# Batches 0 to 2 in 1 KB packets with TensorE transposes, a fixed order of loads, casting weight loads and a later FFN, in an attention and FFN kernel

## The chip, the cores and the metric

The kernel runs on one core of one Trainium2 chip. The metric is device time in microseconds (us) of one execution; lower is better.

Engine names in the profile: PE is TensorE's matmuls, PEld its weight loads, DVE is VectorE, ACT is ScalarE, POOL is GpSimd, SP is SyncE, which here only issues DMAs. "L293" is line 293 of that run's kernel, so line numbers differ from kernel to kernel.

## The reference

Block-causal attention for 8 batches of 8 heads, 576 tokens and 64 channels, then a gated FFN over all 4,608 tokens.

```python
scores = (q @ k.transpose(0, 1, 3, 2)) / sqrt(64)        # q, k, v: (8, 8, 576, 64) float32
scores = where(block_i >= block_j, scores, -1e9)         # blocks of 64 tokens
attn = softmax(scores);  x = (attn @ v).transpose(0, 2, 1, 3).reshape(4608, 512)
out = (maximum(x @ w_gate, 0) * (x @ w_val)) @ w_out     # 512 -> 1536 -> 512
```

## The kernel before

All matmuls are in bf16. The work of attention is cut in 32 *pairs* (two heads of a batch; pair r is head pair r % 4 of batch r // 4). The FFN is a generator of 1,296 matmuls of 512 columns, 144 for each batch and 144 for the collected 64-token tails, and `ffn(n)` sends the next n of them between the pieces of attention. Only TensorE's program order is written by hand; the order on the other engines is made by the scheduler of the language, which ranks the instructions when the program is built.

Batch 0 is loaded as float32 on the SP queue and cast by VectorE; batches 1 to 7 come through casting DMAs from GpSimd's queue and DMA transposes. In both, a packet is one token of one head, 256 B in HBM. Weights are loaded as float32 and cast by whichever engine the scheduler picks.

```python
def load_batch(b):                       # batches 1 to 7
    m, tl = new_bf()                     # bufs=1
    for t, src in enumerate((q, k, v)):
        for c in range(NCH):
            ...
            nc.gpsimd.dma_start(dst, src[b, :, 128*c : 128*c+n, :].rearrange("h p d -> p h d"))
        if t < 2:
            nc.sync.dma_start_transpose((qTm, kTm)[t][b % 2]..., m[t]...)
            ...
def to_xT_dma(r):                        # result of a pair, transposed for the FFN
    nc.sync.dma_start_transpose(xT_of(b)[:, hp, :]..., xnat[:, 0:4, :]...)
...
m0, t0 = load_first_batch()
for i in range(4): load_w_in(i)          # float32 on SP, then nc.any.tensor_copy
...                                      # pairs 0 to 3, with TensorE transposes
load_batch(1)
for i in range(3): load_w_out(i)
ffn(64)
for r in range(4, 4 * B):
    a = [2, 2, 2, 4] if b == 1 else [8, 4, 8, 16]
    scores_1(r); ffn(a[0])
    if r > 4: head_av(r-1, 0); ffn(a[1]); head_av(r-1, 1); to_xT_dma(r-1)
    else: ffn(a[1])
    if hp == 0 and b + 1 < B: load_batch(b + 1)
    ffn(a[2]); scores_2(r); ffn(a[3])
```

The softmax here doesn't subtract the row's maximum and nothing guards it: scores larger than these inputs give would overflow.

Of the kernel before, what the change touches and what calls it, by code (L numbers as in the profile page):

```python
# [10 lines left out]
FP = mybir.dt.float32  # L11
BF = mybir.dt.bfloat16
# [5 lines left out]
def kernel(  # L18
# [10 lines left out]
    nc = tc.nc  # L29

    B, H, S, D = q.shape
# [12 lines left out]
    sb = ctx.enter_context(tc.tile_pool(name="sb", bufs=1))  # L44
# [10 lines left out]
    ident = consts.tile([128, 128], BF)  # L55
# [13 lines left out]
    for i in range(2):  # L69
# [4 lines left out]
        nc.gpsimd.memset(v_bf[i][:, 0:4, :, 64:65], 1.0)  # L74
        nc.gpsimd.memset(v_bf[i][0:64, 4, :, 64:65], 1.0)


    def new_bf():
        m = [sb.tile([128, 4, 512], BF, name=n, bufs=1) for n in ("q_bf", "k_bf")]
        t = [sb.tile([64, 512], BF, name=n, bufs=1) for n in ("q_bt", "k_bt")]  # L80
        return m, t

    def load_first_batch():
        m, tl = new_bf()
        for hp in range(4):
            st = sb.tile([128, 3, 5, 128], FP, name="stage", bufs=4)
            hs = slice(128 * hp, 128 * hp + 128)
            for t, src in enumerate((q, k, v)):
                for hh in range(2):
                    nc.sync.dma_start(  # L90
                        st[:, t, 0:4, 64 * hh : 64 * hh + 64],
                        src[0, 2 * hp + hh, 0:512, :].rearrange(
                            "(c p) d -> p c d", p=128
                        ),
                    )
                nc.sync.dma_start(
                    st[0:64, t, 4, :].rearrange("p (h d) -> p h d", h=2),
                    src[0, 2 * hp : 2 * hp + 2, 512:576, :].rearrange("h p d -> p h d"),
                )
                if t < 2:  # L100
                    nc.vector.tensor_copy(m[t][:, :, hs], st[:, t, 0:4, :])
                    nc.vector.tensor_copy(tl[t][:, hs], st[0:64, t, 4, :])
                else:
                    h2 = slice(2 * hp, 2 * hp + 2)
                    sv = st[:, t, :, :].rearrange("p c (h d) -> p c h d", h=2)
                    nc.vector.tensor_copy(v_bf[0][:, 0:4, h2, 0:64], sv[:, 0:4])
                    nc.vector.tensor_copy(v_bf[0][0:64, 4, h2, 0:64], sv[0:64, 4])
        return m, tl

    def load_batch(b):  # L110
        m, tl = new_bf()
# [16 lines left out]
                )  # L128
                nc.sync.dma_start_transpose((qTt, kTt)[t][b % 2][:, 0:4, :], tl[t])  # L129

    def load_w_in(i):
        for dst, src in ((wg, moe_w_gate), (wv, moe_w_val)):
            st = sb.tile([128, 4, 384], FP, name="stage", bufs=4)
            nc.sync.dma_start(
                st,
                src[:, 384 * i : 384 * (i + 1)].rearrange("(c p) f -> p c f", p=128),
            )
            nc.any.tensor_copy(dst[i], st)

    def load_w_out(i):  # L140
        st = sb.tile([128, 4, 512], FP, name="stage", bufs=4)
        nc.sync.dma_start(
            st,
            moe_w_out[512 * i : 512 * (i + 1), :].rearrange("(c p) f -> p c f", p=128),
        )
        nc.any.tensor_copy(wo[i], st)


    def pe_transposes(hp, m, tl):
        hs = slice(128 * hp, 128 * hp + 128)  # L150
        for t in range(2):
            tp = psum_ffn.tile([128, 1024], BF, name="ffnp")
            for c in range(4):
                nc.tensor.transpose(
                    tp[:, 128 * c : 128 * c + 128], m[t][:, c, hs], ident
                )
            nc.tensor.transpose(tp[:, 512:576], tl[t][:, hs], ident[:64, :64])
            nc.vector.tensor_copy(
                (qTm, kTm)[t][0][:, :, hp, :],
                tp[:, 0:512].rearrange("p (c n) -> p c n", c=4),  # L160
            )
            nc.vector.tensor_copy((qTt, kTt)[t][0][:, hp, :], tp[:, 512:576])

    def scores(b, hp, pieces):
        sc = psum_sc.tile([128, 2, 512], FP, name="sc")
        for pos, c, main in pieces:
            for hh in range(2):
                ps = slice(64 * hh, 64 * hh + 64)
                n = 512 - 128 * c if main else 64
                o = sc[:, hh, pos : pos + n]  # L170
                if main:
                    o = o.rearrange("p (c n) -> p c n", n=128)
                nc.tensor.matmul(  # L173
                    o,
                    kTm[b % 2][ps, c, hp, :]
                    if c < 4
                    else kTt[b % 2][ps, hp : hp + 2, :].rearrange("p h n -> p (h n)"),
                    qTm[b % 2][ps, c:4, hp, :] if main else qTt[b % 2][ps, hp, :],
                    start=True,
                    stop=True,  # L180
                )
        return sc
# [12 lines left out]
    def scores_2(r):  # L195
        b, hp = divmod(r, 4)
        at = attnT[r % 2]
        sc = scores(b, hp, [(0, 2, True)] + [(256 + 64 * c, c, False) for c in range(4)])
        nc.scalar.activation(at[:, :, 1024:1536], sc, AF.Exp, scale=scale)  # L199
        nc.vector.memset(at[64:128, :, 1024:1088], 0.0)  # L200
        sc = scores(b, hp, [(0, 4, False)])
        nc.scalar.activation(
            at[0:64, :, 1536:1600], sc[0:64, :, 0:64], AF.Exp, scale=scale
        )
# [4 lines left out]
    def head_av(r, hh):  # L209
        b, hp = divmod(r, 4)  # L210
        h = 2 * hp + hh
        at = attnT[r % 2]
        vb = v_bf[b % 2]
        if hh == 0:
            xnats[r] = sb.tile([128, NCH, 128], BF, name="xnat", bufs=3)
        xnat = xnats[r]
        av = psum_av.tile([128, NCH, 65], FP, name="av")
        for p in range(NCH):
            for c in range(p + 1):
                col = BASE[c] + 128 * (p - c) if p < 4 else TAIL + 64 * c  # L220
                nc.tensor.matmul(  # L221
                    av[:, p, :],
                    at[:, hh, col : col + 128],
                    vb[:, c, h, :],
                    start=(p == 0),
                    stop=(c == p),
                    skip_group_check=True,
                )
        recip = sb.tile([128, NCH], FP, name="recip", bufs=4)
        nc.vector.reciprocal(recip, av[:, :, 64])  # L230
        nc.vector.tensor_tensor(  # L231
            out=xnat[:, :, 64 * hh : 64 * hh + 64],
            in0=av[:, :, 0:64],
            in1=recip.to_broadcast([128, NCH, 64]),
            op=AX.mult,
        )
# [16 lines left out]
    def to_xT_dma(r):  # L253
        b, hp = divmod(r, 4)
        xnat = xnats[r]
        nc.sync.dma_start_transpose(
            xT_of(b)[:, hp, :].rearrange("p (c n) -> p c n", c=4),
            xnat[:, 0:4, :].rearrange("p c n -> p (c n)"),
        )
        nc.sync.dma_start_transpose(xTt[:, hp, b : b + 1, :], xnat[0:64, 4, :])  # L260
# [60 lines left out]
    def ffn(n):  # L321
        for _ in range(n):
            if next(gen, 0) == 0:
                return


    m0, t0 = load_first_batch()
    for i in range(4):
        load_w_in(i)

    with tc.manual_schedule(engines={mybir.EngineType.PE}):
        pe_transposes(0, m0, t0)
        for r in range(4):
            scores_1(r)
            if r < 3:
                pe_transposes(r + 1, m0, t0)
            if r > 0:
                head_av(r - 1, 0)
                head_av(r - 1, 1)
            scores_2(r)  # L340
            if r > 0:
                to_xT_pe(r - 1)
        head_av(3, 0)
        head_av(3, 1)
        to_xT_pe(3)
        load_batch(1)
        for i in range(3):
            load_w_out(i)
        ffn(64)
        for r in range(4, 4 * B):  # L350
            b, hp = divmod(r, 4)
            a = [2, 2, 2, 4] if b == 1 else [8, 4, 8, 16]
            scores_1(r)
            ffn(a[0])
            if r > 4:
                head_av(r - 1, 0)
                ffn(a[1])
                head_av(r - 1, 1)
                to_xT_dma(r - 1)
            else:  # L360
                ffn(a[1])
            if hp == 0 and b + 1 < B:
                load_batch(b + 1)
            ffn(a[2])
            scores_2(r)
            ffn(a[3])
        head_av(4 * B - 1, 0)
        ffn(4)
        head_av(4 * B - 1, 1)
        to_xT_dma(4 * B - 1)  # L370
        ffn(10**6)
# [30 lines left out]
```

## Time and profile before

Three runs took 443.13 to 447.69 us, median 444.28; the profiled execution spans 445.2 us.

The page of the kernel before: TensorE's busy time, its busy tenths in 40 slices of 11.1 us, the granted clock in tenths, the busy share of the DMA engines in tenths, and the two data queues (packets, MB, share of 16 engines).

```profile
PE 374.7 (84%) x2844; PEld 180.5 (41%) x2892; DVE 174.8 (39%) x459; ACT 169.6 (38%) x243; POOL 90.8 (20%) x117
...
PE   1467957866199979997999699989999999999995
...
PEclk9999998799599999999999879999999999999999
DMA  9989999999990599059905990492013002002004
...
q0 software_dynamic: 98448, 12.39, 50.0%
q1 hardware_dynamic: 76528, 34.82, 36.2%
```

TensorE is mostly at 9 tenths from slice 11 on (counted from 0), with dips, and mostly below it before. The DMA engines are nearly full for the first 130 us; over the span q0, which casts 256 B to 128 B in each packet, takes half of their time for a quarter of the bytes written (12.39 of 47.66 MB; the page counts a casting packet by its size after the cast). The waits view of the same kernel (who waited for whom: us in total, times, longest):

```profile
PE ffnp L271 <- DMA xT<-xnat: 25.0, 5, 14.2
...
PE sc L173 <- DMA kTm_89<-k_bf: 5.1, 1, 5.1
```

and two lines of its timeline of TensorE (start, us, instruction; in brackets the idle time before it and what ended it):

```profile
106.29 0.81 PE L271 MATMUL ffnp<-xT,wg_75 128*128 128x512 bf16 x3
121.29 0.59 PE L271 MATMUL ffnp<-xT,wg_75 128*128 128x512 bf16 x1 [14.18 <-DMA xT<-xnat]
```

The FFN of batch 1 stood 14.18 us before its fourth matmul, for a transposed result (xT) that came by DMA. Four more such waits came later, of 2.46, 2.58, 3.81 and 1.96 us. The trace's clock records show half rate from 110.3 us, during the long wait, for 13.7 us, and again from 164.9, 209.3 and 253.7 us, at the first three of the later ones, for 3.4, 3.4 and 6.8 us; at the last the record stayed full.

One caution about the clock row: it shows 9 in the first slices because the trace has no clock record before 48.9 us. The matmuls suggest half rate there: four FFN matmuls took 1.75 us at 47.41 us and 1.03 us from 49.00 on.

To follow the time I read the start of the first score matmul of some pairs from the timelines:

| start, us | before |
|---|---|
| pair 0 | 11.97 |
| pair 3 | 35.94 |
| first FFN matmul | 46.13 |
| pair 4 (batch 1) | 66.31 |
| pair 8 (batch 2), 104 FFN matmuls sent | 92.72 |
| pair 12 (batch 3), 248 FFN matmuls sent | 150.71 |
| end | 445.2 |

### The profile page before, as it was taken

To read this page: it belongs to the slowest core of one execution; us is meant where nothing else is said; L and a number is where in the kernel's file an instruction comes from. 1 tells how busy PE (TensorE), PEld (TensorE's weight loads), DVE (VectorE), ACT (ScalarE), POOL (GpSimd) and SP (SyncE) were. 2 spreads that over 40 slices of the span, in tenths; PEclk is the share of its full clock that TensorE was granted. 3 is DMA by queue.
4 is the path that set the end of the run, shared out by engine and by line. 5 is a ranking of instruction groups with operands and counts; after the bars stand their busy time and mean duration, and the time that the engine had idled before them with its cause. 6 is when DMAs were issued, how large, how long until landed. Compare 5 with 4: busy or idle time off the path is not lost.

```text
span 445.2 us, 7281 instructions
## 1 busy us (share of the span) xinstructions
PE 374.7 (84%) x2844; PEld 180.5 (41%) x2892; DVE 174.8 (39%) x459; ACT 169.6 (38%) x243; POOL 90.8 (20%) x117
## 2 busy tenths in 40 slices
PE   1467957866199979997999699989999999999995
PEld 0245423332044434443444244434444444444442
DVE  2565522531044424442444134424444453433331
ACT  1427415732045334533453245425534550330320
POOL 5034333154600181027102610030000000000000
PEclk9999998799599999999999879999999999999999
DMA  9989999999990599059905990492013002002004
GB/s 137 176 253 238 263 155 303 169 132 132 185 95 15 96 179 127 15 113 167 124 13 115 154 134 15 74 157 65 15 38 92 19 16 84 26 0 94 1 0 94
DMA packets 175010, 47.66 MB, mean 107 GB/s; under 512 B 164737, under 2 KB 168833, under 8 KB 174977
## 3 DMA queue, kind: packets, MB, share of 16 engines
q0 software_dynamic: 98448, 12.39, 50.0%
q1 hardware_dynamic: 76528, 34.82, 36.2%
q8 instruction: 22, 0.36, 0.3%
q14 instruction: 12, 0.09, 0.1%
HBM read 37.75 MB, written 9.44 MB: 106 GB/s over the span
## 4 chain that ended last, share of the span: by engine, by line
PE 62%; DMA 20%; issue 5%; SPq 4%; ACT 3%; DVE 3%; POOL 1%; DVEq 0%; ACTq 0%
PE ffnp L283 19%; PE ffnp L271 17%; PE ffnp L299 15%; DMA xT<-xnat 9%; PE av L221 6%; PE sc L173 5%; DMA k_bf<-in_k_dram 5%; DMA stage<-in_moe_w_out_dram 2%; SPq L125 2%; DMA stage<-in_q_dram 2%; DMA xTt<-xnat 2%; DVE xnat L231 1%; SPq L129 1%; SPq L90 1%; ACT gate_sb L280 1%
## 5 line engine op out<-in xcount | busy, mean ns | idle before, releaser
L280 ACT ACTIVATE gate_sb<-ffnp 128x512 bf16<-128x512 f32 x108 | 64.4, 596 | 153.2 <-PE ffnp L271 153.1
L293 DVE TENSOR_TENSOR hT<-gate_sb,ffnp 128x512 bf16<-128x512 bf16 x108 | 74.3, 688 | 84.5 <-PE ffnp L283 79.6
L299 PEld LDWEIGHTS <-hT 128*128 128x128 bf16 x432 | 39.6, 98 | 45.6 <-issue 2.5
L120 POOL DMA_DIRECT2D q_bf<-in_q_dram x28 | 24.5, 892 | 150.9 <-DMA qTm_86<-q_bf 77.1
L271 PE MATMUL ffnp<-xT,wg_75 128*128 128x512 bf16 x89 | 26.1, 405 | 25.8 <-DMA xT<-xnat 25.0
L309 DVE COPY ob<-ffnp 128x512 f32<-128x512 f32 x36 | 24.9, 692 | 38.1 <-PE ffnp L299 24.6
L221 PEld LDWEIGHTS <-attnT_94 128*128 128x128 bf16 x480 | 21.5, 108 | 42.8 <-issue 28.9
L299 PE MATMUL ffnp<-wo_85,hT 128*128 128x512 bf16 x142 | 36.8, 380 | 0.2
L299 PE MATMUL ffnp<-wo_84,hT 128*128 128x512 bf16 x137 | 35.5, 380 | 0.6
L299 PE MATMUL ffnp<-wo_83,hT 128*128 128x512 bf16 x137 | 35.6, 379 | 0.1
L231 DVE TENSOR_TENSOR xnat<-av,recip 128x320 bf16<-128x320 f32 x64 | 31.5, 491 | 4.4 <-DMA xTt<-xnat 2.3
L199 ACT ACTIVATE attnT_94<-sc 128x1024 bf16<-128x1024 f32 x16 | 16.3, 1021 | 36.8 <-PE sc L173 36.8
L283 PE MATMUL ffnp<-xT,wv_79 128*128 128x512 bf16 x96 | 28.7, 428 | 0.0
L188 ACT ACTIVATE attnT_94<-sc 128x1024 bf16<-128x1024 f32 x16 | 16.4, 1023 | 32.2 <-PE sc L173 32.2
L230 DVE RECIPROCAL recip<-av 128x5 f32<-128x5 f32 x64 | 12.3, 193 | 36.9 <-PE av L221 35.9
L120 POOL DMA_DIRECT2D k_bf<-in_k_dram x28 | 24.8, 900 | 8.4 <-DMA kTm_89<-k_bf 4.9
L221 PEld LDWEIGHTS <-attnT_95 128*128 128x128 bf16 x480 | 18.8, 102 | 17.9 <-DVE xnat L231 14.2
L271 PE MATMUL ffnp<-xT,wg_77 128*128 128x512 bf16 x89 | 25.1, 390 | 0.4
L283 PE MATMUL ffnp<-xT,wv_82 128*128 128x512 bf16 x93 | 25.3, 389 | 0.1
L283 PE MATMUL ffnp<-xT,wv_81 128*128 128x512 bf16 x96 | 25.1, 383 | 0.0
L271 PE MATMUL ffnp<-xT,wg_78 128*128 128x512 bf16 x90 | 24.6, 391 | 0.3
L271 PE MATMUL ffnp<-xT,wg_76 128*128 128x512 bf16 x90 | 24.4, 380 | 0.3
(103 smaller groups left out, 423.4 us busy)
## 6 DMA issues: line engine op xcount, KB each, us to landing
out_dram<-ob SPq DMA_DIRECT2D x32, 256.0 KB, 5.7
q_bf<-in_q_dram POOLq DMA_DIRECT2D x28, 128.0 KB, 6.8
k_bf<-in_k_dram POOLq DMA_DIRECT2D x28, 128.0 KB, 9.2
stage<-in_moe_w_gate_dram SPq DMA_DIRECT2D x4, 768.0 KB, 7.7
stage<-in_moe_w_val_dram SPq DMA_DIRECT2D x4, 768.0 KB, 8.5
stage<-in_moe_w_out_dram SPq DMA_DIRECT2D x3, 1024.0 KB, 10.9
v_bf_97<-in_v_dram POOLq DMA_DIRECT2D x16, 128.0 KB, 7.5
v_bf_96<-in_v_dram POOLq DMA_DIRECT2D x12, 128.0 KB, 11.6
```

What stands on the lines that cost most here:

```text
L120: nc.gpsimd.dma_start(dst, src[b, :, 128 * c : 128 * c + n, :].rearrange("h p d -> p h d"),)
L173: nc.tensor.matmul(o, kTm[b % 2][ps, c, hp, :] if c < 4 else kTt[b % 2][ps, hp : hp + 2, :].rearrange("p h n -> p (h n)"), qTm[b % 2][ps, ...
L188: nc.scalar.activation(at[:, :, 0:512], sc, AF.Exp, scale=scale)
L199: nc.scalar.activation(at[:, :, 1024:1536], sc, AF.Exp, scale=scale)
L221: nc.tensor.matmul(av[:, p, :], at[:, hh, col : col + 128], vb[:, c, h, :], start=(p == 0), stop=(c == p), skip_group_check=True,)
L231: nc.vector.tensor_tensor(out=xnat[:, :, 64 * hh : 64 * hh + 64], in0=av[:, :, 0:64], in1=recip.to_broadcast([128, NCH, 64]), op=AX.mult,)
L271: nc.tensor.matmul(gate, wg[i][:, c, fo : fo + 128], x[:, c, :], start=(c == 0), stop=(c == 3),)
L280: nc.scalar.activation(gate_sb, gate, AF.Relu)
L283: nc.tensor.matmul(val, wv[i][:, c, fo : fo + 128], x[:, c, :], start=(c == 0), stop=(c == 3),)
L293: nc.vector.tensor_tensor(out=h, in0=gate_sb, in1=val, op=AX.mult)
L299: nc.tensor.matmul(op, hT[f][:, 128 * s : 128 * (s + 1)], wo[f // 4][:, f % 4, :], start=(f == 0), stop=(f == 11),)
L309: nc.vector.tensor_copy(ob, op)
```

## The change

The intent: feed TensorE earlier and without gaps. Batches 0 to 2 are staged as float32, q and k with four tokens (1 KB) in a packet, and transposed by TensorE; the casts of staged batches are on VectorE. Loads wait for one another in a fixed order: batch 0, input weights, batch 1, output weights, batch 2; a load that waits for an earlier one is called *gated* below. Weights are cast by the DMA itself. The results of pairs 4 to 7 are transposed by TensorE too, instead of by DMA. The FFN runs 20 of its matmuls later (a pair of the steady part sends 36).

```diff
+    def after(ins, other):               # a wait on another engine's or DMA's completion
+        if other is not None: tc.add_manual_dep(ins.ins, other.ins.name, SYNC)
+        return ins
-        m = [sb.tile([128, 4, 512], BF, name=n, bufs=1) for n in ("q_bf", "k_bf")]
+        m = [sb.tile([128, 4, 512], BF, name=n, bufs=2) for n in ("q_bf", "k_bf")]
-    def load_first_batch(): ...          # 256 B packets, batch 0 only
+    def early_load(b, per, gate=None):   # batches 0 to 2
+        ...
+        for h0 in range(0, 8, per):
+            for t, src in enumerate((q, k)):
+                st = new_stage(256 * per)
+                i = nc.sync.dma_start(st.rearrange("p (h n) -> p h n", h=per),
+                    src[b, h0:h1, 0:512, :].rearrange("h (p j) d -> p h (j d)", j=4))
+                after(i, gate)
+            ...
+            for t in range(2):
+                nc.vector.tensor_copy(m[t][...], sts[t]...)       # the cast
+            ... v in 256 B packets, one DMA a head, after(i, gate), cast -> mark
+    def load_w_in(i, gate=None):
-            nc.sync.dma_start(st, ...); nc.any.tensor_copy(dst[i], st)
+            ins = nc.gpsimd.dma_start(dst[i], ...); after(ins, gate)
     ...  load_w_out likewise
-    def pe_transposes(hp, m, tl):
+    def pe_transposes(b, hp, m, tl):     # copies out of PSUM now interleave four tokens
     ...
-    m0, t0 = load_first_batch()
+    *early[0], marks0 = early_load(0, 2)
     for i in range(4):
-        load_w_in(i)
+        w_in = load_w_in(i, marks0[2])
     ...
-        load_batch(1)
+        *early[1], marks1 = early_load(1, 4, w_in)
-            load_w_out(i)
+            w_out = load_w_out(i, marks1[0])
-        ffn(64)
+        ffn(76)
-            a = [2, 2, 2, 4] if b == 1 else [8, 4, 8, 16]
+            a = {1: [2, 2, 4, 6], 2: [4, 4, 4, 12]}.get(b, [8, 4, 8, 16])
     ...
-                to_xT_dma(r - 1)
+                to_xT_pe(r - 1) if r <= 8 else to_xT_dma(r - 1)
+            early_load(2, 4, w_out) at pair 4; pe_transposes of the next pair after scores_3(r)
```

The FFN's place in numbers: at pair 12 the kernel before has sent 248 FFN matmuls, the changed one 228. The cut leaves out a small change of order: `scores_2` is split in two, and in batch 0's rounds a pair's second head product moves behind the first part.

More of the change, by code (lines that the diff above doesn't have):

```diff
@@ L75 @@
         nc.gpsimd.memset(v_bf[i][0:64, 4, :, 64:65], 1.0)
+    SYNC = mybir.DependencyInfo(
+        mybir.DependencyClass.Sync, mybir.DependencyReason.DATA
+    )
+    def after(ins, other):
+        if other is not None:
+            tc.add_manual_dep(ins.ins, other.ins.name, SYNC)
+        return ins
     def new_bf():
-        m = [sb.tile([128, 4, 512], BF, name=n, bufs=1) for n in ("q_bf", "k_bf")]
-        t = [sb.tile([64, 512], BF, name=n, bufs=1) for n in ("q_bt", "k_bt")]
+        m = [sb.tile([128, 4, 512], BF, name=n, bufs=2) for n in ("q_bf", "k_bf")]
+        t = [sb.tile([64, 512], BF, name=n, bufs=2) for n in ("q_bt", "k_bt")]
@@ L81, in new_bf, with new_stage @@
         return m, t
-    def load_first_batch():
+    def new_stage(w):
+        return sb.tile([128, 2048], FP, name="stage", bufs=5)[:, 0:w]
+    def early_load(b, per, gate=None):
         m, tl = new_bf()
-        for hp in range(4):
-            st = sb.tile([128, 3, 5, 128], FP, name="stage", bufs=4)
-            hs = slice(128 * hp, 128 * hp + 128)
-            for t, src in enumerate((q, k, v)):
-                for hh in range(2):
-                    nc.sync.dma_start(
-                        st[:, t, 0:4, 64 * hh : 64 * hh + 64],
-                        src[0, 2 * hp + hh, 0:512, :].rearrange(
-                            "(c p) d -> p c d", p=128
-                        ),
-                    )
-                nc.sync.dma_start(
-                    st[0:64, t, 4, :].rearrange("p (h d) -> p h d", h=2),
-                    src[0, 2 * hp : 2 * hp + 2, 512:576, :].rearrange("h p d -> p h d"),
-                )
-                if t < 2:
-                    nc.vector.tensor_copy(m[t][:, :, hs], st[:, t, 0:4, :])
-                    nc.vector.tensor_copy(tl[t][:, hs], st[0:64, t, 4, :])
-                else:
-                    h2 = slice(2 * hp, 2 * hp + 2)
-                    sv = st[:, t, :, :].rearrange("p c (h d) -> p c h d", h=2)
-                    nc.vector.tensor_copy(v_bf[0][:, 0:4, h2, 0:64], sv[:, 0:4])
-                    nc.vector.tensor_copy(v_bf[0][0:64, 4, h2, 0:64], sv[0:64, 4])
-        return m, tl
@@ new lines, in early_load, with tail @@
+        st_t = new_stage(1536)
+        marks = []
+        def tail(t, src):
+            i = nc.sync.dma_start(
+                st_t[0:64, 512 * t : 512 * t + 512].rearrange("p (h d) -> p h d", h=8),
+                src[b, :, 512:576, :].rearrange("h p d -> p h d"),
+            )
+            after(i, gate)
+        for h0 in range(0, 8, per):
+            h1 = h0 + per
+            sts = []
+            for t, src in enumerate((q, k)):
+                st = new_stage(256 * per)
+                i = nc.sync.dma_start(
+                    st.rearrange("p (h n) -> p h n", h=per),
+                    src[b, h0:h1, 0:512, :].rearrange("h (p j) d -> p h (j d)", j=4),
+                )
+                after(i, gate)
+                sts.append(st)
+            if h0 == 0:
+                tail(0, q)
+                tail(1, k)
+            for t in range(2):
+                nc.vector.tensor_copy(
+                    m[t][:, :, 64 * h0 : 64 * h1].rearrange("p j (h d) -> p h j d", d=64),
+                    sts[t].rearrange("p (h j d) -> p h j d", h=per, j=4),
+                )
+                if h0 == 0:
+                    nc.vector.tensor_copy(tl[t], st_t[0:64, 512 * t : 512 * t + 512])
+            st = new_stage(256 * per)
+            for h in range(per):
+                i = nc.sync.dma_start(
+                    st[:, 256 * h : 256 * h + 256].rearrange("p (c d) -> p c d", c=4),
+                    v[b, h0 + h, 0:512, :].rearrange("(c p) d -> p c d", p=128),
+                )
+                after(i, gate)
+            if h0 == 0:
+                tail(2, v)
+            mark = nc.vector.tensor_copy(
+                v_bf[b % 2][:, 0:4, h0:h1, 0:64].rearrange("p c h d -> p h c d"),
+                st.rearrange("p (h c d) -> p h c d", h=per, c=4),
+            )
+            marks.append(mark)
+            if h0 == 0:
+                nc.vector.tensor_copy(
+                    v_bf[b % 2][0:64, 4, :, 0:64],
+                    st_t[0:64, 1024:1536].rearrange("p (h d) -> p h d", h=8),
+                )
@@ L110, in load_batch @@
+        return m, tl, marks
     def load_batch(b):
@@ L129, in load_batch, with load_w_out @@
                 nc.sync.dma_start_transpose((qTt, kTt)[t][b % 2][:, 0:4, :], tl[t])
-    def load_w_in(i):
+    def load_w_in(i, gate=None):
         for dst, src in ((wg, moe_w_gate), (wv, moe_w_val)):
-            st = sb.tile([128, 4, 384], FP, name="stage", bufs=4)
-            nc.sync.dma_start(
-                st,
+            ins = nc.gpsimd.dma_start(
+                dst[i],
                 src[:, 384 * i : 384 * (i + 1)].rearrange("(c p) f -> p c f", p=128),
             )
-            nc.any.tensor_copy(dst[i], st)
-    def load_w_out(i):
-        st = sb.tile([128, 4, 512], FP, name="stage", bufs=4)
-        nc.sync.dma_start(
-            st,
+            after(ins, gate)
+        return ins
+    def load_w_out(i, gate=None):
+        ins = nc.gpsimd.dma_start(
+            wo[i],
             moe_w_out[512 * i : 512 * (i + 1), :].rearrange("(c p) f -> p c f", p=128),
         )
-        nc.any.tensor_copy(wo[i], st)
-    def pe_transposes(hp, m, tl):
+        return after(ins, gate)
+    def pe_transposes(b, hp, m, tl):
         hs = slice(128 * hp, 128 * hp + 128)
@@ L152, in pe_transposes @@
             tp = psum_ffn.tile([128, 1024], BF, name="ffnp")
-            for c in range(4):
+            for j in range(4):
                 nc.tensor.transpose(
-                    tp[:, 128 * c : 128 * c + 128], m[t][:, c, hs], ident
+                    tp[:, 128 * j : 128 * j + 128], m[t][:, j, hs], ident
                 )
@@ L158, in pe_transposes @@
             nc.vector.tensor_copy(
-                (qTm, kTm)[t][0][:, :, hp, :],
-                tp[:, 0:512].rearrange("p (c n) -> p c n", c=4),
+                (qTm, kTm)[t][b % 2][:, :, hp, :].rearrange("p c (n j) -> p c n j", j=4),
+                tp[:, 0:512].rearrange("p (j c n) -> p c n j", j=4, c=4),
             )
-            nc.vector.tensor_copy((qTt, kTt)[t][0][:, hp, :], tp[:, 512:576])
+            nc.vector.tensor_copy((qTt, kTt)[t][b % 2][:, hp, :], tp[:, 512:576])
     def scores(b, hp, pieces):
@@ L200, in scores_2, with scores_3 @@
         nc.vector.memset(at[64:128, :, 1024:1088], 0.0)
+    def scores_3(r):
+        b, hp = divmod(r, 4)
+        at = attnT[r % 2]
         sc = scores(b, hp, [(0, 4, False)])
@@ L324, in ffn @@
                 return
-    m0, t0 = load_first_batch()
+    early = {}
+    *early[0], marks0 = early_load(0, 2)
     for i in range(4):
-        load_w_in(i)
+        w_in = load_w_in(i, marks0[2])
     with tc.manual_schedule(engines={mybir.EngineType.PE}):
-        pe_transposes(0, m0, t0)
+        pe_transposes(0, 0, *early[0])
         for r in range(4):
@@ L335 @@
             if r < 3:
-                pe_transposes(r + 1, m0, t0)
+                pe_transposes(0, r + 1, *early[0])
             if r > 0:
                 head_av(r - 1, 0)
+            scores_2(r)
+            if r > 0:
                 head_av(r - 1, 1)
-            scores_2(r)
+            scores_3(r)
             if r > 0:
@@ L345 @@
         to_xT_pe(3)
-        load_batch(1)
+        *early[1], marks1 = early_load(1, 4, w_in)
         for i in range(3):
-            load_w_out(i)
-        ffn(64)
+            w_out = load_w_out(i, marks1[0])
+        ffn(76)
         for r in range(4, 4 * B):
             b, hp = divmod(r, 4)
-            a = [2, 2, 2, 4] if b == 1 else [8, 4, 8, 16]
+            a = {1: [2, 2, 4, 6], 2: [4, 4, 4, 12]}.get(b, [8, 4, 8, 16])
+            if r == 4:
+                pe_transposes(1, 0, *early[1])
             scores_1(r)
@@ L358 @@
                 head_av(r - 1, 1)
-                to_xT_dma(r - 1)
+                if r <= 8:
+                    to_xT_pe(r - 1)
+                else:
+                    to_xT_dma(r - 1)
             else:
                 ffn(a[1])
-            if hp == 0 and b + 1 < B:
+            if hp == 0 and b == 1:
+                *early[2], _ = early_load(2, 4, w_out)
+            elif hp == 0 and b + 1 < B:
                 load_batch(b + 1)
@@ L365 @@
             scores_2(r)
+            scores_3(r)
+            if r + 1 < 12:
+                pe_transposes(*divmod(r + 1, 4), *early[(r + 1) // 4])
             ffn(a[3])
```

## The prediction

> # Prediction
>
> **What bounds the kernel now.** TensorE, but not all the time: busy 374.7 us of 445.2 (page, engine table). By the windows view it idles 20.1 us in 0 to 40, 10.9 in 40 to 80, 17.2 in 80 to 120, and some 22 in the rest. In steady state a head pair with 36 FFN matmuls takes 9.95 us (timeline, 140.8 to 150.7), one FFN matmul 0.216. Three places are not TensorE-bound:
>
> 1. Start. Batch 0 comes in 256 B packets; its last k is cast at 29.96 us, the FFN starts at 46.1 (timeline). Packet records: 256 B takes 24 ns, 1536 B 79, casting 256 B to 128 B 37. Batch 1's v (4,608 casting packets, about 10 us of all 16 queues) goes out at 3.3 us, in the middle of this.
> 2. Batch 1 is late: 5.1 us wait for kTm at 61 us, then only 10 FFN matmuls a pair, 6.6 us each.
> 3. Waits for xT<-xnat DMA: 25.0 us in five (waits view), 14.2 of it at 107 us. [...]
>
> **What the change does.**
>
> - q and k of batches 0 to 2 in 1 KB packets, about 54 ns each (estimate, interpolated). Batch 0: 2,048 of these and 5,632 of 256 B, 17 to 20 us of all queues instead of 30. [...]
> - Rounds of batch 0 then run on their own chain (6.5 to 8 us): FFN starts near 37 us, gain 9.
> - Weights cast by DMA: takes casts of 1.0 to 1.5 us off ACT and DVE, but a casting packet may take 80 to 160 ns (estimate), 20 to 41 us for the input weights. Batch 1 is gated on their last, w_out on batch 1, batch 2 on w_out: this chain is the risk.
> - Batch 1's first scores near 55 us, after 76 FFN matmuls, instead of 66.3 after 64.
> - Added TensorE transposes: 8 calls of 0.55 us and 4 of 0.28, 5.5 us (estimate); their VectorE copies make batch 1 VectorE-heavy (about 7 us of 7.5 a pair).
> - The FFN crosses into the next batch 20 matmuls later: 4.3 us and other work, 5.6 in all. The later waits were 2 to 3 us each, so they vanish, with the half clock behind them (about 15 us together).
>
> **Sum.** Pair 12 begins at 150.7 us now, with 248 FFN matmuls done; then near 119 with 228. Then 20 pairs of 9.95 are 199, 348 matmuls left are 75, the end 7: 400. I add 8 for waits of the gated loads, PSUM buffers shared with transposes, and DMA contention while batch 3 loads: **408 us, range 397 to 424**. Chances: faster 0.94, same 0.05, slower 0.01.
>
> **What would show it.** FFN start near 37 us; batch 1's first scores near 55; no FFN wait for xT over 1 us after 130, granted clock 1.0 there; TensorE busy near 92%; packets under 512 B down by about 24,600.
>
> **What would make it wrong.** Casting weight packets of 160 ns or more, so that the FFN waits for weights and batches 1 and 2 come late; VectorE queueing in batch 1; batch 3 late at pair 12; xT waits that stay because SP's queue delays them, not the FFN's place.

Two passages are cut from this text, and marked: a reading of the granted clock with a rule for it, and a rule for packet sizes, which no trace of this case shows as they stood. No term of the sum is cut: it came to 400 us, and with 8 for waits to 408. Three figures in it are my estimates: the 15 us for the later waits (the trace before shows 10.8 us of waits there, and 13.7 us at half rate); the 80 to 160 ns for a casting packet (a plain one of 1536 B took 79, and nothing showed the upper end); and VectorE's 7 of 7.5 us a pair in batch 1 (4.9 of 7.7 from pair 4 to pair 8 in the changed kernel).

## The result and the profile after

The changed kernel took 421.56 us (median of four runs, 421.27 to 423.74) against 445.18 (443.13 to 447.69) for the kernel before in the same rounds. The ratio is 0.948, with a 95% interval of 0.942 to 0.954. Ratios here are the mean time of one kernel's fast runs over that of the other's in the same rounds, so not quite the ratio of the medians. Runs of either kernel more than 1.5% above its fastest are told slow and stay out of the ratios; none of these four is.

The page of the changed kernel, the same lines:

```profile
PE 373.0 (89%) x2941; PEld 181.5 (43%) x2992; DVE 192.9 (46%) x503; ACT 161.7 (39%) x237; POOL 73.4 (17%) x98
...
PE   2672796887899999999999999999999999999995
...
PEclk9955599999999999999999999999999999999999
DMA  8998989239999999299539304920021002002004
...
q0 software_dynamic: 76128, 13.57, 48.2%
q1 hardware_dynamic: 68112, 29.51, 32.5%
```

From slice 11 on TensorE is at 9 tenths without a dip until the last slice, and the clock is full from slice 5 on (the first two slices have no clock record; the records show half from 21.1 to 51.8 us). In the first 50 us it is no better than before. The waits view of TensorE in the changed kernel:

```profile
PE ffnp L293 <- DVE xnat L276: 13.9, 8, 8.2
PE av L266 <- DVE xnat L276: 12.2, 16, 1.9
...
PE ffnp L316 <- DVE hT L338: 2.1, 1, 2.1
```

The waits for xT are gone. In their place one wait of 8.2 us for VectorE stands out. The pairs show where the time was gained (the last column is e6, an experiment below). At pair 8 the changed kernel and e6 have sent 132 FFN matmuls, the kernel before 104; 28 of them are 6.0 us of TensorE at 0.216 us each. The ends are spans of the profiled executions.

| start, us | before | predicted | after | e6 |
|---|---|---|---|---|
| pair 0 | 11.97 | | 9.58 | 9.92 |
| pair 3 | 35.94 | | 30.01 | 29.58 |
| first FFN matmul | 46.13 | 37 | 47.66 | 39.46 |
| pair 4 | 66.31 | 55 | 70.44 | 59.17 |
| pair 8 | 92.72 | | 101.22 | 89.19 |
| pair 12 | 150.71 | 119 | 137.73 | 125.71 |
| from pair 12 to the end | 294.5 | 281 | 282.3 | 282.2 |
| end | 445.2 | 408 | 420.0 | 407.9 |

Up to pair 12 the changed kernel is 13.0 us ahead, but with 20 FFN matmuls fewer (20 times 0.216 is 4.3 us), so 8.7 us of real gain. From pair 12 on it needs 12.2 us less although it has those 4.3 us more to do: 16.5 us. The two together are the 25.2 us between the profiled spans. So two thirds of the gain is in the steady part, and the early part, where most of the change was made and where I expected some 27 us, gave 8.7. Nearly all of that lies between pairs 8 and 12, where the kernel before had its 14.18 us wait (e5 below parts this further).

What happened between pair 3 and the FFN is in VectorE's timeline of the changed kernel:

```profile
32.30 0.49 DVE L276 TENSOR_TENSOR xnat<-av,recip 128x320 bf16<-128x320 f32 x1
32.86 0.11 DVE L233 MEMSET attnT_95<- 64x64 uint32 x1
32.93 0.11 DVE L234 MEMSET attnT_95<- 64x64 uint32 x1
39.30 0.69 DVE L125 CAST q_bf<-stage 128x1024 bf16<-128x1024 f32 x1 [6.25 <-DMA stage<-in_q_dram]
...
40.20 0.20 DVE L275 RECIPROCAL recip<-av 128x5 f32<-128x5 f32 x1
41.05 0.69 DVE L125 CAST k_bf<-stage 128x1024 bf16<-128x1024 f32 x1 [0.65 <-DMA stage<-in_k_dram]
41.66 0.48 DVE L276 TENSOR_TENSOR xnat<-av,recip 128x320 bf16<-128x320 f32 x1
```

The cast of batch 1's q waited 6.25 us for its DMA, and everything behind it waited too: the reciprocal at 40.20 and the normalising multiply (xnat) at 41.66 belong to pair 2, whose matmuls had ended at 33.8 us. So nothing overtook the cast here: a 0.20 us reciprocal was held for over 6 us by a cast it has nothing to do with. That is what "in-order" says of this queue below. The chain of work over this stretch, followed back (start, us, what):

```profile
20.81 14.47 DMA wv_82<-in_moe_w_val_dram
...
35.33 0.37 SPq L115
...
35.80 5.22 DMA stage<-in_k_dram
...
41.05 0.69 DVE k_bf L125
41.75 0.41 DVE xnat L276
...
42.20 0.61 PE ffnp L293 x4
```

The cast waited for its load; the load was gated on the last weight (wv_82), which landed at 35.3 us; and the scheduler had ranked the cast ahead of work that was ready at 33.8.

### The profile page after: what moved, and what is told of

Read it like the earlier page. It is cut to its first block, busy times and chain, and to the rows that moved or that the text cites. A ratio compares the mean times of both kernels' runs of the same rounds, so it can differ in the third digit from the quotient of the medians.

```text
span 420.0 us, 7452 instructions
## 1 busy us (share of the span) xinstructions
PE 373.0 (89%) x2941; PEld 181.5 (43%) x2992; DVE 192.9 (46%) x503; ACT 161.7 (39%) x237; POOL 73.4 (17%) x98
## 4 chain that ended last, share of the span: by engine, by line
PE 75%; DMA 7%; DVE 6%; issue 5%; ACT 4%; SPq 2%; POOL 1%; ACTq 0%; DVEq 0%
PE ffnp L344 22%; PE ffnp L328 20%; PE ffnp L316 19%; PE av L266 6%; PE sc L214 6%; DMA wv_82<-in_moe_w_val_dram 3%; DVE xnat L276 2%; DMA stage<-in_v_dram 2%; DMA stage<-in_k_dram 1%; PE ffnp L195 1%; ACT attnT_95 L232 1%; ACT gate_sb L325 1%; ACT attnT_95 L229 1%; DVE recip L275 1%; SPq L133 1%
## 5 line engine op out<-in xcount | busy, mean ns | idle before, releaser
L344 PE MATMUL ffnp<-wo_84,hT 128*128 128x512 bf16 x141 | 36.6, 379 | 0.2
L162 POOL DMA_DIRECT2D q_bf<-in_q_dram x20 | 17.6, 894 | 82.9 <-PE ffnp L198 44.9
L240 ACT ACTIVATE attnT_95<-sc 128x1024 bf16<-128x1024 f32 x16 | 16.4, 1022 | 33.0 <-PE sc L214 33.0
L240 ACT ACTIVATE attnT_94<-sc 128x1024 bf16<-128x1024 f32 x16 | 16.4, 1024 | 31.5 <-PE sc L214 31.5
L316 PE MATMUL ffnp<-xT,wg_77 128*128 128x512 bf16 x95 | 24.6, 380 | 2.2 <-DVE hT L338 2.1
L266 PEld LDWEIGHTS <-attnT_94 128*128 128x128 bf16 x480 | 18.5, 101 | 18.5 <-DVE xnat L276 14.8
L316 PE MATMUL ffnp<-xT,wg_75 128*128 128x512 bf16 x94 | 25.6, 394 | 0.4 <-issue 0.3
L328 PE MATMUL ffnp<-xT,wv_79 128*128 128x512 bf16 x90 | 25.3, 391 | 0.3
L316 PE MATMUL ffnp<-xT,wg_78 128*128 128x512 bf16 x96 | 24.8, 379 | 0.4 <-DVE qTt_91 L203 0.4
L266 PEld LDWEIGHTS <-attnT_95 128*128 128x128 bf16 x480 | 18.8, 102 | 14.5 <-DVE xnat L276 11.0
L328 PE MATMUL ffnp<-xT,wv_82 128*128 128x512 bf16 x87 | 24.2, 380 | 0.6 <-issue 0.2
L229 ACT ACTIVATE attnT_95<-sc 128x1024 bf16<-128x1024 f32 x16 | 16.4, 1023 | 21.7 <-PE sc L214 21.7
L316 PE MATMUL ffnp<-xT,wg_76 128*128 128x512 bf16 x94 | 24.6, 380 | 0.1
L328 PE MATMUL ffnp<-xT,wv_81 128*128 128x512 bf16 x89 | 24.4, 380 | 0.4
L328 PE MATMUL ffnp<-xT,wv_80 128*128 128x512 bf16 x91 | 24.4, 379 | 0.3
```

The lines of the kernel that those rows point to most:

```text
L162: nc.gpsimd.dma_start(dst, src[b, :, 128 * c : 128 * c + n, :].rearrange("h p d -> p h d"),)
L229: nc.scalar.activation(at[:, :, 0:512], sc, AF.Exp, scale=scale)
L240: nc.scalar.activation(at[:, :, 1024:1536], sc, AF.Exp, scale=scale)
L266: nc.tensor.matmul(av[:, p, :], at[:, hh, col : col + 128], vb[:, c, h, :], start=(p == 0), stop=(c == p), skip_group_check=True,)
L316: nc.tensor.matmul(gate, wg[i][:, c, fo : fo + 128], x[:, c, :], start=(c == 0), stop=(c == 3),)
L328: nc.tensor.matmul(val, wv[i][:, c, fo : fo + 128], x[:, c, :], start=(c == 0), stop=(c == 3),)
```

## The experiments

Twelve kernels ran, all with correct results. e1 to e4 ran, and a0, e5, e6 and e7, on the same chip; e9 to e12 on another chip. (There is no e8.) Where I compare e9 to e12 with e6, I compare positions in the profiles, and times only loosely.

Theory A: VectorE's queue, in-order as in the trace above (the cast's wait of 6.25 us), with casts of gated loads ranked too early, ate the gain. Rival B: the gated chain of loads delivers batches 1 and 2 too late in any case, so nothing done about VectorE helps.

### e1 and e2: the casts of batch 1 (and 2) ranked behind batch 0's work

```diff
-        to_xT_pe(3)
-        *early[1], marks1 = early_load(1, 4, w_in)
+        x3 = to_xT_pe(3)                                   # its last copy
+        *early[1], marks1 = early_load(1, 4, w_in, x3)     # each cast after x3
 e2 also: batch 2's casts after the copies of pe_transposes(1, 0)
```

> The changed kernel, with one more ordering: the VectorE casts of batch 1 must stand behind the last VectorE copy of batch 0 (xT and xTt of pair 3). Theory A (VectorE's in-order queue: the cast of batch 1's q stood in front of pair 2's reciprocal and waited 6.25 us for a gated load, so TensorE idled 8.2 us and stayed at half clock): FFN starts at 39 to 41 us instead of 47.7, no TensorE wait over 3 us between 20 and 45 us, total 412 to 416 instead of 421.6. Rival B (the gated load chain decides: batch 1 arrives late whatever VectorE does, so the gain is lost again before pair 4): FFN starts earlier but TensorE waits for batch 1 before pair 4 and the total stays within 2 us of 421.6.

> As e1, and the casts of batch 2 stand behind the VectorE copies of batch 1's first transposes. Theory A: the second block (VectorE 3.5 us at 60.8 us waiting for batch 2's q, TensorE 2.1 us) goes too; 1 to 3 us less than e1, 410 to 414. Rival B: no less than e1, since batch 2's data then come later and pair 8 waits for them.

Measured: e1's three fast runs took 420.38, 423.83 and 423.95 us. Its profiled run took 759.53 us and is put aside: in the timelines read from it four FFN matmuls took 1.84 to 2.17 us, against 1.02 to 1.04 in the changed kernel from 51.8 us on, and no run shows the cause. e2 took 421.55 us (421.22 to 421.73). Neither gains anything on the control a0 (421.74), so both totals miss what theory A expected and stand about where rival B put them. Yet e2's profile shows the mechanism of A at the first place: the FFN starts at 40.28 us instead of 47.66, and pair 4 at 64.02 instead of 70.44. By pair 8 the lead is gone (101.23 against 101.22). The VectorE timeline of e2 says where:

```profile
56.36 0.70 DVE L142 CAST v_bf<-stage 128x1024 bf16<-128x1024 f32 x1 [3.77 <-DMA stage<-in_v_dram]
...
68.19 0.11 DVE L239 MEMSET attnT<- 64x64 uint32 x1
70.52 0.70 DVE L142 CAST v_bf<-stage 128x1024 bf16<-128x1024 f32 x1 [2.21 <-DMA stage<-in_v_dram]
71.39 0.42 DVE L149 CAST v_bf<-stage 64x512 bf16<-64x512 f32 x1 [0.18 <-DMA stage<-in_v_dram]
71.73 0.68 DVE L203 COPY qTm<-ffnp 128x512 bf16<-128x512 bf16 x1
...
72.62 0.19 DVE L207 COPY qTt<-ffnp 128x64 bf16<-128x64 bf16 x1
```

and TensorE's timeline of e2 has the answering waits:

```profile
57.71 1.02 PE L321 MATMUL ffnp<-xT,wg 128*128 128x512 bf16 x4 [2.46 <-DVE hT L343]
...
72.87 1.03 PE L321 MATMUL ffnp<-xT,wg 128*128 128x512 bf16 x2 [3.28 <-DVE qTt L207]
```

The block moved. Casts of batch 1's and batch 2's v still stood in front of FFN products and transposed copies, waiting 3.77 and 2.21 us for loads; TensorE waited 2.46 and 3.28 us, and its clock was halved at 72.8 and again at 96.7 us, for 3.4 us each (clock records of the trace; two FFN matmuls at 72.87 us took the 1.03 us that four take at full rate). So after e2 both theories were open: either VectorE's queue still, or the loads.

### e3: batch 1 without its gate

```diff
-        *early[1], marks1 = early_load(1, 4, w_in)
+        *early[1], marks1 = early_load(1, 4)
```

> The changed kernel with batch 1's loads no longer gated on the last input weight. Theory A: the casts of batch 1 still stand in front of batch 0's work on VectorE, but their data come earlier, so the block shrinks to under 3 us; weights land some 10 us later than at 35 us, still in time for the FFN near 41; total 412 to 418. If the gate was needed (rival): the FFN waits for weights or batch 0's last group comes late, total 421 or more.

Measured: 429.76 us (429.28 to 431.31), slower than the changed kernel. The FFN starts at 53.13 us. VectorE's timeline in e3:

```profile
41.42 0.70 DVE L140 CAST v_bf<-stage 128x1024 bf16<-128x1024 f32 x1 [10.10 <-DMA stage<-in_v_dram]
...
58.20 0.70 DVE L140 CAST v_bf<-stage 128x1024 bf16<-128x1024 f32 x1 [5.83 <-DMA stage<-in_v_dram]
```

Without the gate the loads of batch 1 and the weights run together, and casts of v stand in VectorE's queue for 10.10 and 5.83 us. The total is where the rival put it (421 or more), but through VectorE's queue and not through a wait for weights. So taking the gate away is no cure as long as the casts are on VectorE.

### e4 and e5: the place of the FFN alone

```diff
 e4 = before, with
+            if r == 8:
+                a = [4, 2, 4, 6]                 # 16 instead of 36: 20 later from here on
 e5 = after, with
-        ffn(76)
+        ffn(64)
-            a = {1: [2, 2, 4, 6], 2: [4, 4, 4, 12]}.get(b, [8, 4, 8, 16])
+            a = [2, 2, 2, 4] if b == 1 else [8, 4, 8, 16]
```

> The kernel before with only the FFN's place moved: 16 instead of 36 FFN matmuls in pair 8, so that every later pair runs 20 matmuls behind. If the place alone removes the waits for xT: no wait of the FFN for xT over 1 us after 130 us and full clock there, total 427 to 434 instead of 445. If the SP queue keeps xT late: waits of 1 us or more stay and the total is over 438.

> The changed kernel with the FFN back in its old place (64, then 2-2-2-4 and 8-4-8-16). If the later place is worth the same here as in the kernel before (e4: 430.4 against 449.4): waits of the FFN for xT of 2 to 3 us and stretches of half clock come back at each batch border after 130 us, total 434 to 440. If the waits went for another reason (fixed load order, no early casts): no such waits, total within 3 us of 421.6.

Measured: e4 took 430.39 us, ratio to before 0.961 (0.954 to 0.969). TensorE's waits in e4 after 126 us, all of them:

```profile
PE av L221 <- DVE xnat L231: 3.2, 7, 0.5
```

No wait for xT is left, and the clock records show full rate from 126.3 us on, where four FFN matmuls take 1.02 to 1.04 us. From pair 12 to the end e4 takes 429.0 - 146.46 = 282.5 us, like the changed kernel. e5 took 436.17 us against 421.74 for the control a0 in the same rounds, and the waits came back:

```profile
PE ffnp L316 <- DMA xT<-xnat: 8.2, 4, 3.2
```

So letting the FFN stand 20 matmuls later is worth 14.4 us in the changed kernel, and 17 to 19 us (by ratio and by medians) in the kernel before, where the wait at 107 us also became a shorter one of 11.1. e4's expectation was met. e5's was met in its total and its waits, but half clock came back only once after 130 us, from 202.0 to 208.8 us (four FFN matmuls at 204.05 us took 1.90 us).

e5 also shows what the rest of the change did, because it sends as many FFN matmuls by each pair as the kernel before. Up to pair 8 it is behind: 100.23 us against 92.72. From pair 8 to pair 12 it takes 44.5 us where the kernel before took 58.0, and it has no wait for batch 1's xT, whose transposes are on TensorE now. So in the changed kernel the new loading, with the TensorE transposes and the VectorE blocks, cost some 7.5 us by pair 8, and the gain of the early part comes with the vanished 14.18 us wait. The FFN's place didn't remove that one: in e4 11.1 us of it stay. No run changes these transposes alone.

### e6: casts of batches 1 and 2 on GpSimd

```diff
     def early_load(b, per, gate=None):
+        cast = (nc.vector if b == 0 else nc.gpsimd).tensor_copy
-                nc.vector.tensor_copy(     # all casts of early_load
+                cast(
```

GpSimd's queue has little else to do in this stretch, and what it has (the gated weight loads) belongs behind these casts anyway.

> The changed kernel itself, as a control on this chip: 421 to 424 us, FFN start near 47.7 us, the VectorE block at 33 to 39 us in place.

> The changed kernel with the casts of batches 1 and 2 on GpSimd instead of VectorE, so that no cast that waits for a gated load stands in VectorE's queue. In e2 the first block went (FFN start 40.3 instead of 47.7) and the gain was lost by pair 8 to VectorE blocks at 52.6 and 68.3 us. Theory A (VectorE's in-order queue is the whole of it): FFN start 40 to 41, pair 4 at 62 to 64, pair 8 at 93 to 96 instead of 101.2, total 412 to 416. Rival B (the gated chain delivers too late for pairs 4 to 8 anyhow, or GpSimd's casts are too slow): TensorE waits for batch 1 or 2 between 60 and 105 us, pair 8 at 100 or later, total 419 or more.

Measured: e6 took 410.87 us (409.95 to 411.39), 0.921 of before (0.917 to 0.925); the control a0 in the same rounds took 421.74 (421.43 to 423.42). GpSimd's timeline in e6:

```profile
39.46 1.04 POOL L126 CAST q_bf<-stage 128x1024 bf16<-128x1024 f32 x1 [17.52 <-DMA stage<-in_q_dram]
41.32 1.04 POOL L126 CAST k_bf<-stage 128x1024 bf16<-128x1024 f32 x1 [0.83 <-DMA stage<-in_k_dram]
```

The wait for the gated load is now 17.52 us long, on an engine where it stops nobody. TensorE's timeline of e6 at the end of batch 0, and its busy time from the page:

```profile
38.75 0.61 PE L294 MATMUL ffnp<-ident,xnat 128*128 128x128 bf16 x4 [0.81 <-DVE xnat L277]
39.29 0.23 PE L295 MATMUL ffnp<-ident,xnat 64*128 64x64 bf16 x1
39.46 1.89 PE L317 MATMUL ffnp<-xT,wg 128*128 128x512 bf16 x4
```

```profile
PE 373.9 (92%) x2992; PEld 180.8 (44%) x2992; DVE 183.5 (45%) x485; ACT 161.7 (40%) x237; POOL 89.3 (22%) x116
```

The FFN starts at 39.46 us, pair 4 at 59.17 and pair 8 at 89.19; TensorE waits for no staged batch after the start. A GpSimd cast of 128 x 1024 elements takes 1.04 us against 0.69 on VectorE, which does not matter here. VectorE's other work did not get slower beside it: xnat took 492 ns on average in e6 and 491 in the changed kernel. Against the changed kernel the lead is 8.2 us at the start of the FFN, 11.3 at pair 4 and 12.0 at pair 8. Theory A holds in that the casts on VectorE ate the gain, and rival B falls: with the same gates, the data are in time.

e6 takes two things off VectorE, the waiting and the casts' own work (its busy time falls from 192.9 to 183.5 us). At the first block the waiting is most of it: of the 8.18 us that TensorE stood, VectorE stood 5.9 for the loads of q and k. For the whole gain of 10.9 us no run parts the two.

e6 is also the best kernel.

### e7 and e10: the packet size alone

```diff
-                    st.rearrange("p (h n) -> p h n", h=per),
-                    src[b, h0:h1, 0:512, :].rearrange("h (p j) d -> p h (j d)", j=4),
+                for h in range(per):      # 256 B packets, one DMA a head, as v
+                        st[:, 256*h : 256*h + 256].rearrange("p (c d) -> p c d", c=4),
+                        src[b, h0 + h, 0:512, :].rearrange("(c p) d -> p c d", p=128),
 and plain copies out of PSUM.  e7 on the changed kernel, e10 on e6.
```

> The changed kernel with q and k of batches 0 to 2 loaded in 256 B packets, a DMA for each head, as v is (and plain copies out of PSUM). If the 1 KB packets buy the earlier start: first scores 2 to 4 us later than 9.6, each batch's load 5 to 8 us longer, FFN start 2 to 6 us later, total 424 to 432. If packet size hardly matters: within 2 us of the control.

> e6 (casts on GpSimd, 410.9) with q and k of batches 0 to 2 in 256 B packets. e7's comparison had two differences, since VectorE's order also changed. If 1 KB packets buy batch 0's start: FFN over 42. If they only matter for batches 1 and 2, behind the gates: FFN start 39 to 40 as in e6, pair 8 later than 89.2 by 3 to 12 us because batch 2 is late, total 414 to 423. If they don't matter: within 2 us of 410.9.

Measured: e7 took 426.15 us against 421.74. But it starts the FFN at 39.16 us, 8 us earlier than its control (47.10), because the scheduler ranked the casts differently; its VectorE then stood 6.41 us for batch 1's q at 44.8 us. So e7 changes two things. Its total lies in the range expected if 1 KB packets matter (424 to 432), but the later start that this was to come from failed. e10 removes the second change: 412.86 us (410.35 to 413.84), against 410.87 for e6. The FFN starts at 40.20 (e6: 39.46), pair 12 at 125.97 (125.71). Up to there 1 KB packets bought nothing; the 2 us that e10 is behind arise between pairs 12 and 16, where TensorE waits 1.94 us, at 146.97 us, for VectorE's copy into an output buffer (ob). By the changed kernel's packet records 1 KB took 54.0 ns and 256 B 24.5, so the transfer is nearly twice as fast for each byte (0.053 against 0.096 ns); these starts just did not depend on it. Whether the last 2 us belong to the packets I can't say from runs on two chips.

### e9: batch 1's early loads held back, in the kernel before

```diff
+    each DMA of load_batch(1) waits for the cast of batch 0's last v
```

> The kernel before, with batch 1's loads (above all its v, sent at 3.3 us) held until the last v of batch 0 is cast; packets stay at 256 B. e7 showed that 256 B packets cost the start nothing (FFN start 39.2 against 47.1, pair 3 at 29.6). If batch 1's early v is what made batch 0 late in the kernel before: batch 0's last k is cast at 22 to 26 us instead of 30, pair 3 starts at 30 to 32 instead of 35.9, FFN at 40 to 42 instead of 46.1. If the packet form is what matters after all: FFN start stays over 44.

Measured: 450.09 us against 448.06, ratio 1.019 (1.007 to 1.031). That ratio rests on only two of the seven runs of the kernel before, since the other five are told slow; by the medians the two differ by 0.5%. So the total shows no gain, and no sure loss. Batch 0's last k is cast at 25.84 us instead of 29.96, and the FFN starts at 41.30 instead of 46.13, so batch 1's v, the only part of it that was sent so early, was indeed in the way. But TensorE's timeline has this at pair 4:

```profile
67.58 1.03 PE L181 MATMUL sc<-qTm,kTm 64*128 64x512 bf16 x6 [10.17 <-DMA kTm<-k_bf]
```

Batch 1, held back, came 10.17 us too late. The earlier FFN start was worth nothing because the next batch arrived no earlier: the start gained 4.8 us and pair 4 came 1.3 us later than before.

### e11: weights staged and cast by engines, on e6

```diff
-            ins = nc.gpsimd.dma_start(dst[i], ...)
+            ins = nc.sync.dma_start(st, ...); nc.any.tensor_copy(dst[i], st)
 the same for w_out; same gates
```

> e6 with the weights loaded as float32 on the SP queue and cast by VectorE or ScalarE, under the same gates. A casting 1536 B packet took 82 ns in the changed kernel, a plain one 79 in the kernel before, so transfer time is the same; what is left is 1.0 to 1.5 us of cast for each of eleven tiles, and stage buffers shared with the batches. If those casts stand in the way: FFN start 1 to 4 us later, total 412 to 418. If not: within 2 us of 410.9.

Measured: 416.93 us (414.64 to 417.55), FFN start 43.04, pair 8 at 96.85. Two of the casts in e11's timeline:

```profile
22.49 0.96 DVE L182 CAST wg<-stage 128x1536 bf16<-128x1536 f32 x1 [1.41 <-DMA stage<-in_moe_w_gate_dram]
26.13 0.96 DVE L182 CAST wv<-stage 128x1536 bf16<-128x1536 f32 x1 [0.90 <-DMA stage<-in_moe_w_val_dram]
```

They stand in VectorE's queue in the middle of batch 0 and wait there for weights, the same fault again, with the work of the casts on top. So casting in the DMA is worth some 6 us, loosely, since the two ran on different chips. The risk I named did not come: a casting 1536 B packet took 82 ns in the changed kernel, a plain one 79 in the kernel before. The casts that the DMA takes over had taken 0.95 to 1.90 us each on VectorE and ScalarE in the kernel before. On the 256 B packets casting showed more: 36.6 ns in the kernel before and 39.5 in the changed one, against 24.4 and 24.5 plain.

### e12: more FFN matmuls inside pairs 4 to 7, on e6

```diff
-        ffn(76)
+        ffn(60)
-            a = {1: [2, 2, 4, 6], ...
+            a = {1: [4, 4, 4, 6], ...
```

> e6 with 60 instead of 76 FFN matmuls ahead of pair 4 and 18 instead of 14 in each of pairs 4 to 7. In e6 these pairs take 7.5 us each with TensorE waiting for av and xnat. If the pairs are bound by that chain: pair 4 starts 3.5 us sooner (near 55.7) and pair 8 1.5 to 3.5 us sooner, total 407 to 409.5. If they are TensorE-bound or batch 1 comes too late: within 1 us of 410.9.

Measured: 411.41 us (410.44 to 412.13), no gain. Pair 4 started at 57.66, only 1.5 us sooner than in e6 instead of the 3.5 expected, and pair 8 at 91.40, so the four pairs took 33.7 us instead of 30.0: the 16 added matmuls cost their full 3.5 us. The idle time in these pairs was not filled that way.

## Why the prediction was right or wrong

The direction and the range (397 to 424) held; the centre was 13.6 us too low against the median of 421.56. That the range held is partly luck: pair 12 came 18.7 us after the 119 predicted, and the 8 us of slack and a wide range took that in. Point by point:

- **The later FFN: right, and the largest single part.** I expected about 15 us from the waits for xT and the half clock behind them; the steady part gained 16.5 us, e5 shows 14.4 for the place alone (11.5 of it from pair 12 on), e4 at least 17 in the kernel before, and no wait for xT is left. The clock is full there, as expected (1.00 from 120 us on, by the windows view). The rival I had named (SP's queue keeps xT late) falls with e4 for these waits. The long one, at batch 1, the sum counted as gone without naming a reason; it went with the transposes on TensorE.
- **"FFN starts near 37 us, gain 9": wrong, and this is the step that failed.** It started at 47.66, 1.5 us later than before. I took batch 0's rounds to run on their own chain of work. They did, until a cast of batch 1, ranked ahead on VectorE and waiting for a gated load, held them for over 6 us. I had named the gated loads and VectorE's queue as separate risks, and not seen that they act together: here the gate on a load held everything behind its cast in VectorE's queue, for 6.25 us. e6 takes the cast out of that queue and starts at 39.46, 2.5 us from the prediction.
- **Why the start was early at all.** I gave it to 1 KB packets (17 to 20 us of all queues instead of 30). e10 shows nearly the same start with 256 B packets (FFN at 40.20 us against 39.46). e9 shows that batch 1's v, sent at 3.3 us in the kernel before, cost the start 4.8 us: that part of my reading was right, the packet part was not. The packet time itself was well estimated (54 ns, measured 54.0).
- **Batch 1's first scores at 55 us:** 70.44, of which 10.7 us are the late FFN. The rest is a second VectorE block, 3.46 us at 60.8 us for batch 2's q, and half clock until 51.8 us. In e6 it is 59.17.
- **From pair 12 on: 281 us predicted, 282.3 measured.** With e6's pair 12 (125.71) the sum ends at 407.9 us, near the 408 that included 8 us of slack. So the 12 us that the changed kernel's profile lacks go with the casts on VectorE: a0 to e6 is 10.9 us. Even so e6's pair 12 is 6.7 us later than predicted, which uses up most of the slack.
- **Casting weights:** the packet cost stayed at the low end of my estimate (82 of 80 to 160 ns), and TensorE shows no wait for weights.
- **Two smaller figures.** TensorE busy 89% instead of 92 (e6 has 373.9 of 407.9, 92%). Packets under 512 B fell by 36,881 and not 24,600, because I had counted the loads but not the 256 B packets of the DMA transposes that TensorE's transposes replaced (11,520 by the packet records; the rest are 4 B packets).

What stays open: whether 1 KB packets are worth 2 us or nothing, how much of e6's gain is waiting taken off VectorE and how much the work of the casts, and what holds pairs 4 to 7 at 7.5 us in e6.

## What to carry to other kernels

When a load is gated, look at which engine consumes it and what stands behind that consumer: in VectorE's queue here it was held too (a reciprocal ready at 33.8 us ran at 40.20). Put such consumers on a queue whose other work can wait (in e6 a wait of 17.52 us on GpSimd held nobody, and the kernel gained 10.9 us), rather than only pushing them a few places back (e2 moved the block and gained nothing). And when a change has many parts, try the cheapest one alone: in the changed kernel the FFN's place in the schedule, one list of numbers, gave 14.4 us and all the rest together 9.6 (e5 against the kernel before, by medians). Only with e6 did the rest come to more.
